# Refilling VectorE's queue further ahead in the w_out stages of an attention and relu² kernel, with a matmul product moved between the last ones of a stage

## Chip, cores, metric

One core of one Trainium2 chip. The metric is the device time of one execution in microseconds (us), lower is better.

## The reference, cut to what matters

```python
scores = (q @ k.transpose(0, 1, 3, 2)) / sqrt(64)      # B=8, H=12, S=448, D=64
attn   = (maximum(scores, 0) ** 2 / 448) @ v           # relu squared, no softmax
x      = attn.transpose(0, 2, 1, 3).reshape(3584, 768)
h      = x @ w_in                                      # 768 x 2048
g      = maximum(h, 0) ** 2
out    = g @ w_out                                     # 2048 x 768
```

## The kernel before

TensorE (PE) is kept busy with two matrix products, h = x @ w_in and out = g @ w_out, and the pieces of attention for later batches are laid between their matmuls. Both products use a seven-product scheme instead of eight (after Strassen). The other engines work for PE:

- ScalarE (ACT) turns scores into a tile `at` (relu), copies partial sums out of PSUM banks (`m1`, `u2`, `u3`), and copies attention's result into `xt`.
- VectorE (DVE) squares each `at`, does relu and square on parts of `g`, forms the sums `s1` to `s4` that the w_out products read, and the output sums `osb` = bank × constant + a copy.

Attention comes in units: seven tiles `at` of two heads' scores, then `av_unit`, 28 matmuls that need all seven squared. The schedule is fixed when the program is recorded. The recording code keeps a rough model of the time on PE (`at_pe`) and DVE (`at_ve`). DVE's urgent sums are issued where they are written; squares (`due`) and work on g (`due_g`) wait in lists, and `fill(until)` puts them into DVE's queue as long as the model says that they end before `until`. So **the order in DVE's queue is decided at recording time**, by the horizon given to `fill`:

```python
    def flush(rest=True):                  # put all that is left
        for d in (due, due_g) if rest else (due,):
            while d:
                put(d)

    def put(d):
        ready, cost, fn, _ = d.popleft()
        at_ve[0] = max(at_ve[0], at_pe[0], ready) + cost
        fn()

    def fill(until):
        for d in (due, due_g):
            while d and max(at_ve[0], at_pe[0], d[0][0]) + d[0][1] <= until:
                put(d)

    def av_unit():
        ...
        flush(rest=False)                  # squares left over: all of them now
        at_pe[0] += 2.65
        ...                                # 28 matmuls on the seven squared tiles
```

The w_out stage works in groups of two row tiles. A group has seven products of eight matmuls (8 × 384 columns), which add up in two banks, X and Y:

```python
            TAG = {"m1": "a", "u2": "b", "u3": "c"}
            ...
            def end7():                    # after product k = 4
                copy("u3")                 # ScalarE copies bank X
                plus(1, c1, "u3")          # VectorE: waits for that copy
                ...
            products = (                   # k = 0 .. 6
                (X, True, lambda: tile_of(rows[0])[:, LO], b11, end1),
                (Y, True, lambda: tile_of(rows[0])[:, HI], b21, end2),
                (X, False, lambda: ss[2], t2, end6),
                (Y, True, lambda: ss[1], t1, end5),
                (X, False, lambda: ss[3], t3, end7),
                (X, False, lambda: tile_of(rows[1])[:, HI], nt4, end4),
                (Y, False, lambda: ss[4], b22, end3))
            ...
                    if f == KH - 1:        # last matmul of product k
                        end()
                        fill(at_pe[0] + (1.7 if k in (1, 5) else 1.3))
        ...
        for n, ls in enumerate(lists):     # next group's first product
            for k in range(7):             #   between k = 4 and k = 5
                if k == 5 and n + 1 < len(lists):
                    steps += lists[n + 1][0]
                if k > 0 or n == 0:
                    steps += ls[k]
```

Product k = 5 adds to the bank that `copy("u3")` has to read first. In all groups but a stage's last, the next group's first product stands between them and hides the copy: the traced run lists two waits of w_out matmuls for a copy, of 0.64 us each, both in a stage's last group (at 312.11 and 386.96 us).

Of the kernel before, what the change touches and what calls it, by code (L numbers as in the profile page):

```python
# [11 lines left out]
FP32 = mybir.dt.float32  # L12
AF = mybir.ActivationFunctionType
ALU = mybir.AluOpType
# [3 lines left out]
def kernel(  # L18
# [9 lines left out]
    nc = tc.nc  # L28

    B, H, S, D = q.shape  # L30
    NT, DM = out.shape
# [10 lines left out]
    P = 128  # L42
# [6 lines left out]
    HALF = DM // 2  # L49
    NT_PAIR = 2 * S // P  # L50
    KH = NF // 2
# [4 lines left out]
    CO = 2.0 ** -42  # L56
# [109 lines left out]
    def sums_w1(i):  # L166


        op, c = divmod(i, 2)
        lo, hi = slice(0, NM // 2), slice(NM // 2, NM)  # L170
        a11, a12, a21, a22 = (w1[c][:, lo], w1[c][:, hi], w1[c + 2][:, lo],
                              w1[c + 2][:, hi])
        if op < 3:
            wsum[op, c] = late["ws"].tile(
                [P, NM // 2, 512], FP16, name=f"ws{op}{c}", tag=f"ws{op}{c}")
        if op == 0:
            nc.vector.tensor_add(wsum[0, c], a21, a22)
        elif op == 1:
            nc.vector.tensor_sub(wsum[1, c], wsum[0, c], a11)
        elif op == 2:  # L180
            nc.vector.tensor_sub(wsum[2, c], a12, wsum[1, c])
        else:
            nc.vector.tensor_sub(a21, a11, a21)
# [157 lines left out]
    at_pe = [0.0]  # L341
# [12 lines left out]
# [5 lines that stand above are left out]
    def now_ve(cost, lag=0.25):  # L359
        at_ve[0] = max(at_ve[0], at_pe[0] + lag) + cost  # L360
# [39 lines left out]
    def mm_tile(i=None):  # L400
        if i is None:
            mm_no[0] += 1
            i = mm_no[0] % len(big)
        return big[i].tile([P, 512], FP32, name="mm", tag="mm")
# [160 lines left out]
    def store(row, osb, c, eng, eng2=None):  # L565
        pr, tb = row
        for i in range(2):
            b, j = divmod(2 * tb + i, J)
            b += 2 * pr
            (eng2 if eng2 and i else eng).dma_start(  # L570
                out=out[b * S:(b + 1) * S, :].rearrange(
                    "(p j) d -> p j d", j=J)[:, j, c],
                in_=osb[64 * i:64 * i + 64, c])
# [26 lines left out]
        now_ve(0.6)  # L600
        op(to[i], x, y)  # L601

    def o_groups(groups):


        steps = []
        sets = [dict() for _ in groups]

        def group(n, rows, last):
            ss = sets[n]  # L610
            X: list = []
            Y: list = []
            c0, c1 = slice(0, HALF), slice(HALF, DM)
            osb: dict = {}
            keep: dict = {}

            def ahead(i, k=n):
                if k < len(groups) and k > 0:
                    flush_g(2 * B)
                if k < len(groups) and i not in sets[k]:  # L620
                    sums(i, groups[k], sets[k])

            TAG = {"m1": "a", "u2": "b", "u3": "c"}

            def copy(nm):
                t = late["m"].tile([P, S], FP32, name=nm, tag=TAG[nm])
                t = t[:, 0:HALF]
                nc.scalar.activation(out=t, in_=X[0][:, 0:HALF], func=AF.Copy, scale=CO)  # L628
                keep[nm] = t

            def plus(row, c, nm, cc=slice(0, HALF)):
                now_ve(0.5)
                nc.vector.scalar_tensor_tensor(  # L633
                    out=osb[row][:, c], in0=Y[0][:, cc], scalar=CO,
                    in1=keep[nm][:, cc], op0=ALU.mult, op1=ALU.add)

            def new_osb():
                for r in range(2):
                    osb[r] = late["osb"].tile([P, DM], FP32, name="osb", tag=f"osb{r}")

            def end1():
                copy("m1")

            def end2():
                new_osb()
                plus(0, c0, "m1")
                if last:
                    store(rows[0], osb[0], c0, nc.sync)

            def end6():  # L650
                copy("u2")
                ahead(3)

            def end5():
                ahead(4)

            def end7():
                copy("u3")
                plus(1, c1, "u3")
                if last:  # L660
                    store(rows[1], osb[1], c1, nc.sync)

            def end4():
                nc.scalar.activation(out=osb[1][:, c0], in_=X[0][:, 0:HALF],  # L664
                                     func=AF.Copy, scale=CO)
                if last:
                    store(rows[1], osb[1], c0, nc.gpsimd)
                else:
                    store(rows[1], osb[1], slice(0, DM), nc.sync)
                ahead(1, n + 1)  # L670
                ahead(2, n + 1)

            def end3():
                plus(0, c1, "u2")
                if last:
                    store(rows[0], osb[0], c1, nc.sync, nc.scalar)
                else:
                    store(rows[0], osb[0], slice(0, DM), nc.sync)

            products = (  # L680
                (X, True, lambda: tile_of(rows[0])[:, LO], b11, end1),
# [4 lines that stand above are left out]
                (X, False, lambda: tile_of(rows[1])[:, HI], nt4, end4),  # L686
                (Y, False, lambda: ss[4], b22, end3))

            def step(k, f):
                acc, fresh, left, right, end = products[k]  # L690

                def run():
                    if f == 0 and fresh and k != 3:
                        acc[:] = [mm_tile(n % 2)]
                    if f == 0 and k == 0:
                        ahead(1)
                        ahead(2)
                    nc.tensor.matmul(  # L698
                        acc[0][:, 0:HALF], lhsT=left()[:, f], rhs=right[:, f],
                        start=(fresh and f == 0),  # L700
                        stop=(f == KH - 1), skip_group_check=not fresh)
                    if f == KH - 1:
                        end()
                        fill(at_pe[0] + (1.7 if k in (1, 5) else 1.3))
                return run

            return [[(0.1625, step(k, f), ((2 if k == 5 else True) if f == 0 else False))
                     for f in range(KH)] for k in range(7)]

        def pre(i):  # L710
            sums(i, groups[0], sets[0])

        lists = [group(n, rows, rows == LAST) for n, rows in enumerate(groups)]
        for n, ls in enumerate(lists):
            for k in range(7):
                if k == 5 and n + 1 < len(lists):
                    steps += lists[n + 1][0]
                if k > 0 or n == 0:
                    steps += ls[k]
        return steps, pre  # L720

    def o_steps(pr):
        groups = [((pr, i), (pr, i + 1)) for i in (0, 2, 4)]
        if pr % 2 == 1:
            return o_groups(groups + [((pr - 1, 6), (pr, 6))])
        steps, pre = o_groups(groups)
        return steps + [(0.0, lambda: save((pr, 6)), False)], pre

    LAST = ((B // 2 - 2, 6), (B // 2 - 1, 6))
# [41 lines left out]
    T_G = NM * 0.1892  # L771
    T_H = NF * T_G
# [4 lines left out]
    events = []  # L777
# [34 lines left out]
            events.append((begin[pr] - 6 + i, lambda b=2 * pr, i=i: sums_x(b, i)))  # L812
    events.append((at0 + 0.3, lambda: visit([])))

    outs = [o_steps(pr) for pr in range(B // 2)]
    for i in (1, 2):
        events.append((2 * T_H - (3 - i) * T_G, lambda i=i: outs[0][1](i)))

    def pre(pr, i):
        def run():  # L820
            flush_g(2 * pr)
            outs[pr][1](i)
        return run

    steps = [(0.1892, None, False)] * 4 + f0[4:]
    for f in range(1, NF):
# [4 lines left out]
    for pr in range(1, B // 2):  # L831
        for b in (2 * pr, 2 * pr + 1):
            for i0 in (0, 4):
                extra: dict = {}
                if i0 and b % 2 == 0:
                    for p, i in ((9, 0), (9, 1), (13, 2), (13, 3)):
                        extra.setdefault(p, []).append(
                            lambda b=b, i=i: sums_x(b + 1, i))
                if i0 and b % 2 == 1:
                    extra[9] = [pre(pr, 1)]  # L840
                    extra[13] = [pre(pr, 2)]
                steps += h_period(b, i0, extra)
        steps += outs[pr][0]

    clock = 0.0
# [41 lines left out]
```

## Time and profile before

| | before |
|---|---|
| device time, median of the first 3 runs | 394.91 us (393.95 to 395.52) |
| span of the traced run | 394.3 us |
| PE busy / DVE busy / ACT busy | 370.6 / 275.7 / 251.1 us |
| PE waiting for squares | 8.2 us |
| span of the four w_out stages o0, o1, o2, last | 45.5, 50.8, 44.7, 41.8 us |

The page's head and its rows of slices (each digit is the busy share of a fortieth of the span, in tenths; PEclk is the granted clock, in tenths of full speed):

```profile
span 394.3 us, 8786 instructions
...
PE 370.6 (94%) x3592; PEld 231.8 (59%) x3592; DVE 275.7 (70%) x512; ACT 251.1 (64%) x374; POOL 107.3 (27%) x128
...
PE   8889999997989999999899999999698999999994
...
PEclk9899999999899999999999999999989999999999
```

Look at the three weak places of PE's row: a 7 and an 8 at slices 10 and 12 (stage o0), an 8 at 20 (stage o1), and a 6 and an 8 at 29 and 31 (stage o2). The clock's row dips at 11 and 30, just behind the 7 and the 6 (its other dip, at the second slice, lies near the program's start). PE is the bound everywhere else; DVE is idle 30% of the span, so the squares that PE waits for aren't late for lack of time.

### The profile page before, as it was taken

What the parts mean: (1) busy time and instruction counts of PE and PEld (TensorE: products, weight loads), DVE (VectorE), ACT (ScalarE), POOL (GpSimd) and SP (SyncE); (2) the same over time, 40 slices, a digit from 0 to 9 for tenths busy, and PEclk for the clock granted to TensorE, in tenths of its full rate; (3) what the DMA queues carried; (4) which work ended last, traced back from release to release, by engine and by line L of the source; (5) the groups of instructions that cost most, each with busy time, mean ns of one, the idle gap of its engine ahead of it and who ended that gap; (6) DMA issues with size and microseconds to landing.
All of it is one profiled execution on the core that took longest, in us unless ns stands there. A gap on an engine that the chain in (4) does not pass through costs nothing.

```text
span 394.3 us, 8786 instructions
## 1 busy us (share of the span) xinstructions
PE 370.6 (94%) x3592; PEld 231.8 (59%) x3592; DVE 275.7 (70%) x512; ACT 251.1 (64%) x374; POOL 107.3 (27%) x128
## 2 busy tenths in 40 slices
PE   8889999997989999999899999999698999999994
PEld 3444444443444678785455578786344488986662
DVE  1696567996555888795975758988735578996441
ACT  2797995785665898776465588786445686441120
POOL 8445423662441244413043044130000000000001
PEclk9899999999899999999999999999989999999999
DMA  8999999999997999869598999491230320001333
GB/s 121 197 204 204 205 193 145 150 148 116 149 113 152 165 91 111 100 88 72 95 124 123 196 136 93 73 118 25 47 82 6 81 77 2 2 0 38 99 98 89
DMA packets 121000, 42.65 MB, mean 108 GB/s; under 512 B 100800, under 2 KB 117600, under 8 KB 120960
## 3 DMA queue, kind: packets, MB, share of 16 engines
q0 software_dynamic: 82912, 23.01, 58.8%
q1 hardware_dynamic: 37968, 18.98, 25.4%
q8 instruction: 28, 0.46, 0.5%
q14 instruction: 12, 0.10, 0.1%
q10 hardware_dynamic: 80, 0.10, 0.1%
HBM read 45.61 MB, written 11.01 MB: 144 GB/s over the span
## 4 chain that ended last, share of the span: by engine, by line
PE 76%; DVE 8%; ACT 6%; DMA 4%; issue 2%; POOL 1%; POOLq 0%; ACTq 0%; DVEq 0%
PE mm L698 30%; PE mm L549 22%; PE slot L251 8%; PE mm L419 8%; PE slot L316 6%; DMA k<-in_k_dram 4%; DVE at L368 4%; ACT at L255 3%; DVE g L497 1%; DVE s L601 1%; ACT u L628 1%; PE slot L221 1%; DVE osb L633 1%; ACT m L485 1%; DVE g L490 1%
## 5 line engine op out<-in xcount | busy, mean ns | idle before, releaser
L255 ACT ACTIVATE at<-slot 128x896 f16<-128x896 f32 x168 | 146.2, 918 | 35.4 <-PE slot L251 35.4
L368 DVE TENSOR_TENSOR at<-at 128x896 f16<-128x896 f16 x168 | 98.8, 618 | 14.5 <-ACT at L255 14.4
L108 POOL DMA_DIRECT2D qs<-in_q_dram x36 | 35.4, 985 | 127.0 <-DMA qT<-qs 119.3
L698 PEld LDWEIGHTS <-s 128*128 128x128 f16 x448 | 42.6, 99 | 34.4 <-issue 6.7
L251 PE MATMUL slot<-qT,kT 64*64 64x448 f16 x756 | 59.2, 369 | 1.8 <-ACT kT L213 0.5
L549 PEld LDWEIGHTS <-w 128*128 128x128 f16 x576 | 54.5, 98 | 5.1 <-issue 4.7
L633 DVE SCALAR_TENSOR_TENSOR osb<-mm,u 128x384 f32<-128x384 f32 x28 | 15.6, 557 | 51.1 <-ACT u L628 39.4
L698 PEld LDWEIGHTS <-g 128*128 128x128 f16 x336 | 32.2, 100 | 27.9 <-issue 9.3
L549 PE MATMUL mm<-xt,w 128*128 128x224 f16 x432 | 48.1, 259 | 0.0
L549 PEld LDWEIGHTS <-ws 128*128 128x128 f16 x432 | 40.2, 98 | 6.6 <-issue 6.6
L316 PE MATMUL slot<-at,vt 64*64 64x448 f16 x588 | 34.9, 352 | 8.3 <-DVE at L368 8.2
L698 PE MATMUL mm<-b,g 128*128 128x384 f16 x224 | 42.0, 333 | 0.0
L698 PE MATMUL mm<-b,s 128*128 128x384 f16 x224 | 41.8, 330 | 0.0
L698 PE MATMUL mm<-t,s 128*128 128x384 f16 x224 | 39.5, 327 | 0.9 <-DVE s L601 0.9
L419 PE MATMUL mm<-xt,w 128*128 128x448 f16 x192 | 39.6, 353 | 0.3 <-ACT xt L279 0.3
L108 POOL DMA_DIRECT2D ks<-in_k_dram x36 | 35.1, 977 | 11.4 <-DMA b<-in_moe_w_out_dram 5.8
L251 PEld LDWEIGHTS <-kT 64*64 64x64 f16 x756 | 19.9, 107 | 30.3 <-issue 25.4
L570 POOL DMA_DIRECT2D out_dram<-osb x2 | 1.1, 565 | 129.2 <-ACT osb L664 129.2
L549 PE MATMUL mm<-x,ws 128*128 128x224 f16 x288 | 34.2, 259 | 0.9 <-ACT m L485 0.9
L628 ACT ACTIVATE u<-mm 128x384 f32<-128x384 f32 x28 | 13.8, 492 | 33.3 <-PE mm L698 32.1
L322 ACT ACTIVATE xt<-slot 128x896 f16<-128x896 f32 x21 | 19.3, 917 | 20.1 <-PE slot L316 20.1
L316 PEld LDWEIGHTS <-vt 64*64 64x64 f16 x588 | 18.0, 106 | 21.8 <-issue 13.4
(63 smaller groups left out, 408.1 us busy)
## 6 DMA issues: line engine op xcount, KB each, us to landing
out_dram<-osb SPq DMA_DIRECT2D x52, 192.0 KB, 3.1
vt<-in_v_dram POOLq DMA_DIRECT2D x24, 224.0 KB, 6.2
qs<-in_q_dram POOLq DMA_DIRECT2D x36, 112.0 KB, 4.1
ks<-in_k_dram POOLq DMA_DIRECT2D x36, 112.0 KB, 4.6
w<-in_moe_w_in_dram POOLq DMA_DIRECT2D x8, 384.0 KB, 11.6
b<-in_moe_w_out_dram POOLq DMA_DIRECT2D x4, 768.0 KB, 17.1
q<-in_q_dram POOLq DMA_DIRECT2D x6, 224.0 KB, 9.2
k<-in_k_dram POOLq DMA_DIRECT2D x6, 224.0 KB, 9.6
```

What stands on the lines that cost most here:

```text
L108: nc.gpsimd.dma_start(out=t[:, :, hh, :], in_=heads(src, n)[:, hh].rearrange("p (j d) -> p j d", d=D))
L221: nc.tensor.transpose(pss[i][64 * hh:64 * hh + 64, i, j * P:(j + 1) * P], src[:, hh, j * D:(j + 1) * D], ident)
L251: nc.tensor.matmul(ps[c, hh, 0:S], lhsT=kT[r, j, c], rhs=qT[r, :, c], start=True, stop=True)
L255: nc.scalar.activation(out=at, in_=ps[:, :, 0:S], func=AF.Relu, scale=SK)
L316: nc.tensor.matmul(ps[64 * hh:64 * hh + 64, hp, 0:S], lhsT=vt[r, hh, j * D:(j + 1) * D], rhs=at[r, hh, :], start=(j == 0), stop=(j == J - 1))
L322: nc.scalar.activation(out=xts[b][:, 2 * u:2 * u + 2, :], in_=ps[:, :, 0:S], func=AF.Copy, scale=CX)
L368: lambda: nc.vector.tensor_mul(at, at, at), 0))
L419: nc.tensor.matmul(cell[0][:, 0:S], lhsT=w1[f // 4][:, m, (f % 4) * P:(f % 4 + 1) * P], rhs=xts[b][:, m, :], start=(m == 0), stop=(m == NM ...
L549: nc.tensor.matmul(XY[s][y][:, r * Q:(r + 1) * Q], lhsT=left(k, i0 + 2 * s + r, m), rhs=right(k, m), start=(fresh and r == 0 and m == 0), ...
L628: nc.scalar.activation(out=t, in_=X[0][:, 0:HALF], func=AF.Copy, scale=CO)
L633: nc.vector.scalar_tensor_tensor(out=osb[row][:, c], in0=Y[0][:, cc], scalar=CO, in1=keep[nm][:, cc], op0=ALU.mult, op1=ALU.add)
L698: nc.tensor.matmul(acc[0][:, 0:HALF], lhsT=left()[:, f], rhs=right[:, f], start=(fresh and f == 0), stop=(f == KH - 1), skip_group_check=n ...
```

## The change

Its intent has three parts. (1) DVE's spare time in w_out stages goes to squares earlier: larger horizons. (2) In a stage's last group nothing hides the copy ahead of k = 5; six matmuls of the next h (one product of `h_period`) are moved there. (3) The very last group has no next h, so its product k = 5 goes to a free bank Z; VectorE adds up the output from Z, which was a ScalarE copy from X before, and makes one sum more, `u5`; and the last product is done in two halves of 192 columns with their own sums and stores. The diff, cut to its core:

```diff
 (in sums_w1: w_in's sums on DVE, now counted in the model)
+        now_ve(0.9)
-    def o_groups(groups):
+    def o_groups(groups, then):
-            TAG = {"m1": "a", "u2": "b", "u3": "c"}
+            TAG = {"m1": "a", "u2": "c", "u3": "d"}
+
+            AFTER = (1.9, 1.9, 2.8, 3.0, 3.0, 2.8, 1.9)
...
                         end()
-                        fill(at_pe[0] + (1.7 if k in (1, 5) else 1.3))
+                        fill(at_pe[0] + AFTER[k])
...
-                if k == 5 and n + 1 < len(lists):
-                    steps += lists[n + 1][0]
+                if k == 5:
+                    steps += lists[n + 1][0] if n + 1 < len(lists) else then
... (in o_steps)
+        if pr < B // 2 - 1:
+            p = 1 - pr % 2
+            then += periods[2 * pr + 2, 0][6 * p:6 * p + 6]
+            del periods[2 * pr + 2, 0][6 * p:6 * p + 6]
... (the last group: end7 also forms u5 = Y*CO + u2; end4's ScalarE copy is left out there)
             def end4():
+                if last:
+                    plus(1, c0, "u3", acc=Z)
+                    store(rows[1], osb[1], c0, nc.gpsimd)
+                    return
...
+            def end3_part(z):
+                h = HALF // 2
+                cc = slice(z * h, z * h + h)
+                c = slice(HALF + cc.start, HALF + cc.stop)
+                plus(0, c, "u5", acc=W, cc=cc)
+                store(rows[0], osb[0], c, nc.sync, nc.scalar)
...
+                if last and k == 5:
+                    acc, fresh = Z, True
...
+            if last:
+                ls[6] = [(0.0825, step3(z, f), False) for z in range(2) for f in range(KH)]
```

## The prediction

> **What bounds the kernel now.** TensorE (PE) is busy 94% of a 394.3 us span, so only its idle time and its slow time can be won. I first cut the span into stages by what PE runs. There are four w_out stages: o0 (86.3 to 131.8 us), o1 (175.7 to 226.5), o2 (270.8 to 315.5) and a last one (352.5 to 394.3). In them PE idles 3.2, 1.3, 5.5 and 5.2 us; in the three w_in stages between them 0.7, 1.1 and 0. So the reserve lies in the w_out stages. The list of PE's waits over the whole span names it (columns: total us, times, longest):
>
> ```profile
> PE slot L316 <- DVE at L368: 8.2, 15, 3.0
> ...
> PE mm L698 <- ACT u L628: 1.3, 2, 0.6
> ...
> PE mm L698 <- DVE s L601: 0.9, 1, 0.9
> ```
>
> L316 is attention's second product: it reads seven tiles `at`, each squared by VectorE (DVE, L368). PE's timeline in o2 shows one such unit:
>
> ```profile
> 280.68 0.95 PE L316 MATMUL slot<-at,vt 64*64 64x448 f16 x16
> 284.64 0.38 PE L316 MATMUL slot<-at,vt 64*64 64x448 f16 x4 [3.00 <-DVE at L368]
> 285.17 0.38 PE L316 MATMUL slot<-at,vt 64*64 64x448 f16 x4 [0.15 <-DVE at L368]
> 285.71 0.38 PE L316 MATMUL slot<-at,vt 64*64 64x448 f16 x4 [0.15 <-DVE at L368]
> 285.90 0.38 PE L251 MATMUL slot<-qT,kT 64*64 64x448 f16 x4
> 286.21 2.47 PE L698 MATMUL mm<-nt,g 128*128 128x384 f16 x8
> 288.47 2.19 PE L698 MATMUL mm<-b,s 128*128 128x384 f16 x8
> ```
>
> Undisturbed, a tile's four matmuls start 0.19 us after the previous tile's (unit at 177.16, whose next scores start at 178.48, 1.32 us later). This unit needs 5.22 us: 3.9 lost, more than the 3.3 us of idle shown, because single tiles run unpipelined. DVE's timeline says why the squares were late:
>
> ```profile
> 275.68 0.68 DVE L601 TENSOR_TENSOR s<-g,s 128x1024 f16<-128x1024 f16 x1
> 279.05 0.56 DVE L633 SCALAR_TENSOR_TENSOR osb<-mm,u 128x384 f32<-128x384 f32 x1 [2.68 <-ACT u L628]
> 279.52 0.61 DVE L368 TENSOR_TENSOR at<-at 128x896 f16<-128x896 f16 x1
> 280.05 0.62 DVE L497 TENSOR_TENSOR g<-g 128x896 f16<-128x896 f16 x1
> ...
> 283.97 2.76 DVE L368 TENSOR_TENSOR at<-at 128x896 f16<-128x896 f16 x5
> ```
>
> DVE idles 2.68 us at an output sum that waits for a ScalarE copy; squares whose inputs were long ready stand behind it, and behind 3.9 us of other work (280.05 to 283.97). It isn't short of time, its order is wrong.
>
> The third loss is in the last columns of slices of one us (PEclk is the first number after the busy times; 1.00 is full speed):
>
> ```profile
> 285.00:286.00 1.00, 0.69 (x15) 0.25 (x11) 1.00 (x3) 0.00 (x0) 0.00 (x0) 1.00 0.00 0
> 286.00:287.00 1.00, 1.00 (x12) 0.49 (x5) 0.72 (x2) 0.86 (x2) 0.00 (x0) 0.77 0.08 16
> 287.00:288.00 1.00, 1.00 (x5) 0.48 (x4) 0.10 (x1) 0.86 (x2) 0.00 (x0) 0.50 0.00 0
> 288.00:289.00 1.00, 1.00 (x5) 0.46 (x3) 0.52 (x1) 0.28 (x1) 0.00 (x0) 0.50 0.00 0
> 289.00:290.00 1.00, 1.00 (x4) 0.46 (x3) 0.00 (x0) 0.21 (x1) 0.00 (x0) 0.53 0.00 0
> 290.00:291.00 1.00, 1.00 (x8) 0.59 (x7) 0.30 (x1) 0.00 (x0) 0.00 (x0) 1.00 0.66 144
> ```
>
> After the stall PE runs at half clock for about 3.4 us. The same follows o0's first stall (98.8 to 102.1 us) and no other wait in a w_out stage.
>
> [...] Cutting the time before each drop into such windows, I count about 1.8 us idle in the window just ahead of both drops, and at most about 1.5 in windows that no drop followed; an estimate of the limit from this trace. [...] The trace gives 33.81 us for 208 of 384 columns, 162.5 each, and 96.7 ns each for 224; none of 192.
>
> **The change, part by part.** I took each engine's order in both builds, and worked forward with the durations above.
>
> *Squares earlier.* After each product the recording code fills DVE's queue up to a horizon, now 1.9 to 3.0 us in place of 1.3 to 1.7. DVE's instructions are the same in number apart from the last group; in o2's first unit the two pairs of squares and three operations on g now stand ahead of the waiting sum. Loss of each unit before, as start of the seventh tile less the start it would have at 0.19 us per tile, and what I expect after:
> - o0 first: 98.38 − 95.55 = 2.8. Its last two squares are still behind the sum that ends at 95.3; squares at 95.9 and 96.4, so 0.9 stays. Gain 1.9.
> - o0 second: 114.52 − 112.97 = 1.55; its squares precede the sum. Gain 1.5.
> - o1 second: 196.88 − 196.13 = 0.75. Gain 0.7.
> - o2 first: 3.9. DVE from 274.55: two squares 1.07, s3 0.6, three of g 1.4, s4 0.6, two squares 1.07, sum 0.5, s1 and s2 1.3, the last square 0.55: done near 281.7, wanted at 281.8. Gain 3.8.
> - o2 second: 301.78 − 299.67 = 2.1. The two squares behind the sum (298.2) end at 299.3, wanted at 299.5. Gain 2.1.
> - o1: the 0.9 us wait for a sum s: the g work ahead of it moves forward, s2 done near 190 and wanted at 191.2. Gain 0.9.
> Sum 10.9.
>
> *Clock.* If no window keeps 1.8 us of idle, both drops go. o0: eight matmuls took 2.67 us for 1.30 and eight scores 0.79 for 0.50, 1.65 lost. o2: 24 matmuls took 5.69 us for 3.9, 1.75 lost. Sum 3.4.
>
> *A product of the next h ahead of the stage's last pair.* In the last group of a stage nothing stands between the product that ScalarE must copy from its bank and the product that adds to that bank:
>
> ```profile
> 310.00 1.47 PE L698 MATMUL mm<-b,s 128*128 128x384 f16 x8
> 312.11 1.46 PE L698 MATMUL mm<-nt,g 128*128 128x384 f16 x8 [0.64 <-ACT u L628]
> ```
>
> Six h matmuls (6 × 0.097 = 0.58 us) now stand there, moved, not added: gain 0.64 in o2, 0.14 in o1 (gap ahead of 222.07). In o0 the move pulls two visits of attention together: 16 scores, with eight matmuls less between them. Scores have two slots, each freed by a 0.82 us ScalarE step; the queue there is u3, two steps, m1, two steps. I expect PE to wait about 0.3 and 0.6 us for slots, less the 0.14 saved: a loss of 0.7. Behind o1 the first copy m of h is done before ScalarE's `xt`, where PE waited some 0.3 us: gain 0.3. Sum 0.4.
>
> *Last group.* Its sixth product goes to a free bank and PE doesn't wait for the copy: 0.64. DVE gains one sum of 0.56 us beside PE. The last product is cut in two of 192 columns: [...] the final sum is half as wide, about 0.36 us for 0.56 (estimate): 0.2. Two more output transfers of half the size go out; the last still needs some 4 us from issue to the end as now (390.35 to 394.3). Sum 0.8.
>
> All: 10.9 + 3.4 + 0.4 + 0.8 = 15.5 us. For small new waits (a sum that now stands behind squares frees its bank later: in o1 near 187.2 us where PE wants it at 187.8) I take off 1.5: 14 us of 394.9 leaves 381.
>
> **Rivals.**
> 1. *ScalarE takes over as the limit.* For: with PE's stalls gone, its at steps, copies and `xt` come closer together; a DVE on time may only move the wait from squares to L255. Against: in o2 it works 23.6 of 44.7 us, in o0 29.3 of 45.5, and PE waits for at steps 0.5 us in all. If half of the unit losses came back as slot waits: 387.
> 2. *Queue order again.* More squares ahead of the sums make output sums late, and PE waits for banks in place of squares. For: the 0.6 us margin in o1. Against: in most groups the next group's product stands between. It would give back 2 to 4 us: 384.
> 3. *The clock still drops*, because 0.9 us in o0 and the slot waits at its end fall into one window. [...] Against: 0.9 is half of what came before. One drop costs 1.7: 383.
> 4. *Transfers bind once PE is faster.* Against: GpSimd's transfers of q mostly wait for a buffer (119 us behind transposes), and PE waits for no transfer after o0 begins. I give it no weight.
>
> **Range and chances.** 381 as centre. The high end takes rival 2 and one drop together, 386. The low end, 377.5, has all 15.5 us and the o0 slot waits away, with some gaps too short to be listed. Over 2% faster means below 387.0; that needs 8 of 15.5 us, and o2 alone has 8.3. Chances: faster 0.91, within 2% 0.08, slower 0.01.
>
> **What would show it.** PE's wait for squares falls from 8.2 to about 1 us, nearly all in o0's first unit; o2's units take about 1.3 us each; the clock is 1.00 in all of o0 and o2; o2 shrinks from 44.7 to about 36.5 us, o0 from 45.5 to about 41; the ScalarE copy wait of L698 is gone; at o0's end a new slot wait of about 0.9 us appears. DVE's busy time stays at 276 us. It is wrong if PE's waits reappear under L255 or L633, if half clock is still granted in o2 (then its cause isn't the idle before it), or if the w_in stages grow by what the w_out stages lost.

Where a cut is marked, statements on queues, on the clock and on the time of a matmul are taken out. The sum came to 10.9 + 3.4 + 0.4 + 0.8 = 15.5 us, less 1.5 is 14; the halves of the last product were counted as the same time on PE, and that isn't from this trace. "Such windows" are stretches of 3.413 us, as long as each stretch of half clock in that trace (98.80 to 102.21 and 286.53 to 289.95 us in the w_out stages); counted again in them, the idle time just ahead of the two drops is 1.85 and 1.82 us (1.93 ahead of a third, in the front), and 1.49 at most in the other windows up to the last matmul. "Unpipelined" is put for what the listing shows: a tile that had waited took 0.38 us, where tiles without a wait start 0.19 us apart. The prediction doesn't say from what it worked out the 0.36 us for a sum of half the width; the trace of after shows 0.36.

## The result

| | before | after |
|---|---|---|
| device time, median of 4 runs | 395.22 us (393.95 to 396.14) | 378.86 us (378.47 to 379.35) |
| ratio, 95% interval | | 0.9589 (0.9558 to 0.962) |
| span of the traced run | 394.3 us | 377.6 us |

A ratio is the mean time of one kernel's fast runs over that of the other's of the same rounds, so it is not quite the ratio of the medians quoted. All outputs are right.

The change made the kernel 4.1% faster. The page after, the same lines as before:

```profile
span 377.6 us, 8806 instructions
...
PE 363.5 (96%) x3600; PEld 231.3 (61%) x3600; DVE 278.6 (74%) x515; ACT 249.8 (66%) x373; POOL 107.1 (28%) x128
...
PE   7889999999999999999999999999999999999994
...
PEclk9999999999999999999999999999999999999998
```

The weak places in PE's row are gone, and so are the dips of the clock behind them. PE's waits, the two lines of attention's matmuls in the w_out stages (total us, times, longest):

```profile
PE slot L252 <- ACT at L256: 1.2, 4, 0.4
...
PE slot L317 <- DVE at L369: 0.5, 2, 0.4
```

The wait for squares went from 8.2 to 0.5 us, and no wait of the w_out products (now line L729) is listed any more, neither for a copy nor for a sum (a delay of 0.34 us in the last stage isn't in the list; it comes below). The first unit of o2, which took 5.22 us before, in PE's timeline after (start, duration, work):

```profile
270.57 1.48 PE L729 MATMUL mm<-b,g 128*128 128x384 f16 x8
271.97 0.38 PE L252 MATMUL slot<-qT,kT 64*64 64x448 f16 x4
272.33 1.55 PE L317 MATMUL slot<-at,vt 64*64 64x448 f16 x28
273.68 0.38 PE L252 MATMUL slot<-qT,kT 64*64 64x448 f16 x4
274.00 1.48 PE L729 MATMUL mm<-nt,g 128*128 128x384 f16 x8
```

All 28 matmuls run in one group, and the next scores start 1.35 us after the unit's start. DVE's timeline ahead of it shows the new order:

```profile
269.36 0.68 DVE L602 TENSOR_TENSOR s<-g,s 128x1024 f16<-128x1024 f16 x1
269.96 1.15 DVE L369 TENSOR_TENSOR at<-at 128x896 f16<-128x896 f16 x2
271.03 0.55 DVE L636 SCALAR_TENSOR_TENSOR osb<-mm,u 128x384 f32<-128x384 f32 x1
```

Two squares stand between the sum s and the output sum. When DVE gets to the output sum, ScalarE's last copy `u` (270.17 to 270.66 us) has been done for 0.37 us: the line has no wait in brackets, where before there were 2.68 us. The granted clock (after the busy times of the five engines) stays full:

```profile
270.00:274.00 4.00, 4.00 (x54) 1.95 (x53) 3.96 (x9) 3.38 (x6) 0.00 (x0) 1.00 0.53 102
274.00:278.00 4.00, 4.00 (x28) 2.26 (x24) 1.69 (x3) 2.03 (x3) 0.00 (x0) 1.00 0.30 62
```

**Where the time went.** I cut each trace at the first w_out matmul of each w_out stage, and at the last matmul of all. The first segment runs from the start of the span to o0; a segment such as "o0 to o1" has a w_out stage and the w_in stage after it (us):

| | front | o0 to o1 | o1 to o2 | o2 to last | last stage | tail | span |
|---|---|---|---|---|---|---|---|
| before | 86.28 | 89.27 | 95.05 | 81.76 | 37.36 | 4.58 | 394.3 |
| after | 84.39 | 84.84 | 93.02 | 73.28 | 36.93 | 5.14 | 377.6 |
| difference | −1.89 | −4.43 | −2.03 | −8.48 | −0.43 | +0.56 | −16.7 |

The front runs the same instructions in the same order on all engines in both. It took 83.25 to 86.28 us in the 14 traces; in the trace of before PE stood 1.7 us for the load of k, where it stood 0.7 in that of after, and half clock followed for 3.41 us (13.47 to 16.88). The only other traces with half clock in the front, e9 and e12 (both with the change), took 86.20 and 85.97. So its 1.89 us are chance of the one trace, which was a slow run besides: 396.39 us, above the four timed ones. The other five segments give 14.8 us (of which 1.46, in o0, are chance of this trace too, see e6); between the medians of before and after the later rounds show 15.05 and 14.69 us.

### The profile page after: what moved, and what is told of

Its sections match the earlier page's. It is cut to its first block, busy times and chain, and to the rows that moved or that the text cites. A ratio compares the mean times of both kernels' runs of the same rounds, so it can differ in the third digit from the quotient of the medians.

```text
span 377.6 us, 8806 instructions
## 1 busy us (share of the span) xinstructions
PE 363.5 (96%) x3600; PEld 231.3 (61%) x3600; DVE 278.6 (74%) x515; ACT 249.8 (66%) x373; POOL 107.1 (28%) x128
## 4 chain that ended last, share of the span: by engine, by line
PE 81%; ACT 6%; DVE 6%; issue 2%; DMA 2%; POOL 1%; POOLq 0%; ACTq 0%; DVEq 0%
PE mm L729 33%; PE mm L550 23%; PE slot L252 9%; PE mm L420 9%; PE slot L317 7%; ACT at L256 4%; DVE at L369 2%; DMA k<-in_k_dram 2%; PE slot L222 1%; DVE g L491 1%; ACT m L486 1%; DVE xt L283 1%; DVE s L602 1%; DVE g L498 0%; ACT qT L214 0%
## 5 line engine op out<-in xcount | busy, mean ns | idle before, releaser
L729 PEld LDWEIGHTS <-s 128*128 128x128 f16 x440 | 41.7, 98 | 32.0 <-issue 4.3
L252 PE MATMUL slot<-qT,kT 64*64 64x448 f16 x756 | 58.1, 360 | 2.6 <-ACT at L256 1.2
L550 PEld LDWEIGHTS <-w 128*128 128x128 f16 x576 | 54.4, 98 | 5.9 <-issue 5.4
L729 PEld LDWEIGHTS <-g 128*128 128x128 f16 x336 | 31.5, 98 | 24.0 <-issue 5.0
L729 PE MATMUL mm<-b,g 128*128 128x384 f16 x224 | 40.7, 326 | 0.0
L729 PE MATMUL mm<-b,s 128*128 128x384 f16 x216 | 39.6, 326 | 0.1
L729 PE MATMUL mm<-t,s 128*128 128x384 f16 x224 | 39.5, 326 | 0.0
L636 DVE SCALAR_TENSOR_TENSOR osb<-mm,u 128x384 f32<-128x384 f32 (+1 forms) x30 | 16.2, 541 | 31.2 <-ACT u L631 23.0
L252 PEld LDWEIGHTS <-kT 64*64 64x64 f16 x756 | 19.9, 104 | 31.1 <-issue 25.7
L317 PE MATMUL slot<-at,vt 64*64 64x448 f16 x588 | 32.2, 350 | 0.6 <-DVE at L369 0.5
L498 DVE TENSOR_TENSOR g<-g 128x896 f16<-128x896 f16 x48 | 29.7, 619 | 1.1 <-ACT g L501 0.2
L420 PEld LDWEIGHTS <-w 128*128 128x128 f16 x192 | 17.3, 98 | 19.1 <-issue 4.8
```

Source lines behind the costliest of these rows:

```text
L252: nc.tensor.matmul(ps[c, hh, 0:S], lhsT=kT[r, j, c], rhs=qT[r, :, c], start=True, stop=True)
L317: nc.tensor.matmul(ps[64 * hh:64 * hh + 64, hp, 0:S], lhsT=vt[r, hh, j * D:(j + 1) * D], rhs=at[r, hh, :], start=(j == 0), stop=(j == J - 1))
L420: nc.tensor.matmul(cell[0][:, 0:S], lhsT=w1[f // 4][:, m, (f % 4) * P:(f % 4 + 1) * P], rhs=xts[b][:, m, :], start=(m == 0), stop=(m == NM ...
L498: due_g.append((t, 0.54, lambda: nc.vector.tensor_mul(g, g, g), b))
L550: nc.tensor.matmul(XY[s][y][:, r * Q:(r + 1) * Q], lhsT=left(k, i0 + 2 * s + r, m), rhs=right(k, m), start=(fresh and r == 0 and m == 0), ...
L636: nc.vector.scalar_tensor_tensor(out=osb[row][:, c], in0=acc[0][:, 0:cc.stop - cc.start], scalar=CO, in1=keep[nm][:, cc], op0=ALU.mult, op ...
```

## The experiments

**Theory**: the gain is the order of VectorE's queue. PE no longer idles for squares, and with that the half clock behind the stalls goes too. **Rivals**: (a) the moved h product and the last group bring a real share; (b) the clock isn't a consequence of the stall but of something else in the stage; (c) any horizon that is long enough will do, so the numbers in `AFTER` don't matter. Each later table row is cut as above.

### One part at a time

e1: only the horizons (and the `now_ve(0.9)`), on the kernel before.

```diff
+            AFTER = (1.9, 1.9, 2.8, 3.0, 3.0, 2.8, 1.9)
-                        fill(at_pe[0] + (1.7 if k in (1, 5) else 1.3))
+                        fill(at_pe[0] + AFTER[k])
```

> The kernel before with the longer horizons for VectorE's queue alone (and the charge of 0.9 us for the weight sums), no moved product, old last group. Theory (queue order): the five late units and the late sum s of o1 go as in the changed kernel, 10.9 us by the prediction's list, and with them both half-clock stretches, 3.4 us: 14 us (13 to 15) below the kernel before; the waits of 0.64 us for the ScalarE copy stay in o2 and the last stage. Rival (ScalarE or banks were behind the squares): under 8 us.

e2: only the moved h product (the kernel after with old horizons, without `now_ve(0.9)`, and with the old last group).

```diff
-                        fill(at_pe[0] + AFTER[k])
+                        fill(at_pe[0] + (1.7 if k in (1, 5) else 1.3))
... (last group as before)
```

> The kernel before with the product of the next h moved ahead of a stage's last pair (and the tags of the copies renamed), old horizons, old last group. Theory: 0.64 us won in o2, 0.1 to 0.4 around o1's end, about 0.6 lost at the end of o0 by slot waits: within 0.6 us of the kernel before, the units as late as before and half clock twice. Rival (this part opened room for VectorE): over 2 us faster.

e3: only the last group (the kernel after with old horizons, without `now_ve(0.9)`, and with no moved product).

```diff
-                        fill(at_pe[0] + AFTER[k])
+                        fill(at_pe[0] + (1.7 if k in (1, 5) else 1.3))
-        if pr < B // 2 - 1:
+        if False:
```

> The kernel before with the changed last group alone (free bank, last product and its output in two halves). By the prediction: 0.8 us faster. By the trace of the changed kernel, in which PE's part of the last stage shrank by 0.43 us and the time from the last matmul to the end grew by 0.56: 0.1 us slower, so no difference that can be told (within 0.4 us).

Measured, with before at 393.87 us in the same rounds:

| | time | ratio to before (95%) | o0 to o1 | o1 to o2 | o2 to last | last stage | tail |
|---|---|---|---|---|---|---|---|
| e1 horizons | 379.32 | 0.962 (0.959–0.9651) | 84.11 | 93.20 | 74.07 | 37.72 | 4.51 |
| e2 h product | 394.31 | 0.9991 (0.9947–1.0035) | 88.53 | 94.87 | 80.30 | 37.36 | 4.53 |
| e3 last group | 393.93 | 0.9998 (0.9955–1.0041) | 87.80 | 95.06 | 81.71 | 36.58 | 5.10 |

The horizons alone give all of it that the timing can tell: 0.962, where the whole change measured 0.9589 in the first rounds and 0.9632 and 0.9622 in later ones. DVE has 512 instructions in e1 as before, so only their order changed. Rival (a) falls. The `now_ve(0.9)` went with the horizons in every run, so its share isn't known. What is left of PE's waits for w_out and squares in e1:

```profile
PE mm L701 <- ACT u L631: 1.3, 2, 0.6
...
PE slot L317 <- DVE at L369: 0.5, 2, 0.4
```

The squares' wait is as small as in the whole change; the copy's 1.3 us stay, because nothing was moved in front of it. The other two parts do what they should where they should, and lose it again elsewhere. The h product takes 0.79 us off "o2 to last" (74.07 in e1, 73.28 after) and 0.18 off "o1 to o2", and adds 0.73 to "o0 to o1" (84.11 to 84.84). The last group takes 0.78 off the last stage (37.36 to 36.58) and adds 0.52 to the tail.

### Is the clock a consequence of the stall?

e6: the kernel before, but PE does 14 matmuls on zeros ahead of the stalled unit of o2. They write the unit's own PSUM slot, which the unit's first matmuls overwrite. The stall stays; PE is merely not idle in it.

```diff
         ps = slot(FP32)
+        for _ in range(14 if n == 20 else 0):
+            nc.tensor.matmul(ps[:, 0, 0:S], lhsT=zeros[:, 0:P], rhs=zeros,
+                             start=True, stop=True)
```

> The kernel before with 14 dummy matmuls of 448 columns (2.6 us at full clock) ahead of o2's first unit, in the bank that the unit then overwrites. PE can't finish the unit sooner, because the squares come as late as before. Theory (half clock follows PE's idle time in a window): no half clock in o2, 1.7 us faster (1.2 to 2.0). Rival (the drop has another cause, or the dummy work costs time by itself): same time or slower, half clock still there.

Measured: 392.35 us, ratio 0.9952 (0.9918 to 0.9986); "o2 to last" went from 81.76 to 80.08. PE's timeline in e6, the zeros, the end of the unit, and the product after it:

```profile
277.42 2.81 PE L312 MATMUL slot<-zeros 128*128 128x448 f16 x14
...
282.45 0.38 PE L319 MATMUL slot<-at,vt 64*64 64x448 f16 x4 [0.15 <-DVE at L371]
...
282.95 1.47 PE L701 MATMUL mm<-nt,g 128*128 128x384 f16 x8
```

The unit still ends at the pace of the squares (its seventh tile starts 15.11 us after o2's first matmul in both traces), but the product behind it takes 1.47 us where it took 2.47 before. The slices around it, e6 first, then e2, which has the same stall without the zeros:

```profile
280.00:282.00 2.00, 1.58 (x26) 0.69 (x25) 1.97 (x5) 0.00 (x0) 0.00 (x0) 1.00 0.00 0
282.00:284.00 2.00, 1.85 (x19) 0.83 (x19) 1.47 (x3) 1.12 (x2) 0.00 (x0) 1.00 0.04 8
```

```profile
280.00:282.00 2.00, 0.36 (x4) 0.13 (x4) 1.97 (x4) 0.00 (x0) 0.00 (x0) 0.87 0.00 0
282.00:284.00 2.00, 2.00 (x18) 0.56 (x14) 1.73 (x4) 0.66 (x1) 0.00 (x0) 0.50 0.04 8
```

So PE's idleness brings the half clock, and rival (b) falls for o2: 1.68 us of the 8.48 there are clock. It is hardly luck of one trace: the six runs of e6 have a mean granted clock of 0.994 to 0.998 (on the average 0.995), the eleven of before in the same rounds 0.981 to 0.996 (0.988).

The drop in o0 is another matter. In e2, e3 and e6, which have before's order ahead of that place, the clock was 1.00 throughout o0, with the same stalls; "o0 to o1" took 87.80 and 87.81 us in e3 and e6, against 89.27 in the trace of before. And in e2 the half clock of o2 began in the midst of the stall, so that part of it fell on idle time: 80.30 is 81.76 less the 0.79 that the moved product gives in o2 and 0.67 more, so its half clock cost about 1.0 us (estimate: 1.68 − 0.67) in place of 1.68.

The traces show what decides it. In all 14, the changes of the clock lie a whole number of 3.413 us apart (in the trace of before, from the first full clock on, 2, 1, 24, 1, 54, 1 and 30 times that), and where this grid lies against the stage differs from run to run. I cut PE's idle time (with the ends of matmuls as the profile models them) on each trace's own grid, from the first full clock to the last matmul: 1514 windows. The seven with 1.82 to 2.86 us of idle were each followed by a window at half clock, and none of the others, with 1.60 us or less, was. The seven are all the drops there are in this stretch. o0's first stall left 1.85 us in one window in the trace of before, but at most 1.41, 1.60 and 1.29 in e2, e3 and e6. The length of a single gap doesn't tell it: in the trace of before the drop in o0 followed gaps of at most 1.0 us, that in o2 a gap of 3.0 us, and e6, which left 0.57 us idle in the stall of o2, shows no drop there. (Behind the last matmul it is less clear: a window of 1.85 us at e10's end was not followed by one at half clock.) In these traces a stall thus brings half clock or not, and costs more or less, as it happens to lie on the grid. It fits that before's runs scatter over 392.2 to 397.4 us, with a mean granted clock of 0.993 to 0.996 in those under 392.5 and of 0.986 or less in those over 395, the front's share included.

### Does the size of the horizon matter?

e7: the kernel after with one far horizon.

```diff
-            AFTER = (1.9, 1.9, 2.8, 3.0, 3.0, 2.8, 1.9)
+            AFTER = (5.0,) * 7
```

> The changed kernel with a horizon of 5.0 us after every product. Theory (VectorE's queue is a question of order in both directions): where many operations on g are pending, at the starts of o1, o2 and the last stage, they now stand ahead of a sum that frees a bank or feeds the next product; 1 to 4 us slower than the changed kernel, with waits of the w_out matmuls for sums or banks, and o0 (nothing pending on g) unchanged. Rival (the earlier the better): as fast as the changed kernel or faster.

Measured: 381.87 us (381.38 to 383.15), ratio 0.9693 (0.9661 to 0.9725) to before, against 378.84 for the kernel after in the same rounds: 3.0 us slower. "o1 to o2" grew by 1.63, "o2 to last" by 0.78, the last stage by 0.68; o0 stayed. New among PE's waits:

```profile
PE mm L729 <- DVE osb L636: 1.9, 3, 0.9
...
PE mm L729 <- DVE s L602: 1.0, 2, 0.7
```

At the start of o1, PE's timeline:

```profile
175.92 1.46 PE L729 MATMUL mm<-t,s 128*128 128x384 f16 x8 [0.66 <-DVE osb L636]
178.13 1.47 PE L729 MATMUL mm<-b,s 128*128 128x384 f16 x8 [0.75 <-DVE s L602]
```

The sum of the first wait ran on DVE at 175.32, behind nine operations on g that had begun at 171.14 (the first, the last, and the sum):

```profile
171.14 0.44 DVE L496 TENSOR_SCALAR g<-g 128x896 f16<-128x896 f16 x1
...
175.02 0.39 DVE L496 TENSOR_SCALAR g<-g 128x896 f16<-128x896 f16 x1
175.32 0.55 DVE L636 SCALAR_TENSOR_TENSOR osb<-mm,m 128x384 f32<-128x384 f32 x1
```

Rival (c) falls: too short a horizon puts squares behind sums that wait, too long a one puts sums that PE wants behind work with time to spare. This is the prediction's rival 2, and the values of the change avoid nearly all of it.

### What the change loses

Three places were left: 0.9 us in o0's first unit, the slot waits at o0's end, and the tail. o0's first unit after:

```profile
92.52 1.14 PE L317 MATMUL slot<-at,vt 64*64 64x448 f16 x20
94.03 0.38 PE L317 MATMUL slot<-at,vt 64*64 64x448 f16 x4 [0.37 <-DVE at L369]
94.56 0.38 PE L317 MATMUL slot<-at,vt 64*64 64x448 f16 x4 [0.15 <-DVE at L369]
```

The seventh tile starts at 94.56 instead of 92.52 + 6 × 0.19 = 93.66: the 0.9 of the prediction. And o0's end:

```profile
121.13 0.75 PE L550 MATMUL mm<-xt,w 128*128 128x224 f16 x6
122.14 0.38 PE L252 MATMUL slot<-qT,kT 64*64 64x448 f16 x4 [0.26 <-ACT at L256]
122.95 0.38 PE L252 MATMUL slot<-qT,kT 64*64 64x448 f16 x4 [0.43 <-ACT at L256]
```

e4: no moved product in o0.

```diff
-        if pr < B // 2 - 1:
+        if 0 < pr < B // 2 - 1:
```

> The changed kernel without the moved product at the end of o0 (kept in o1 and o2). Theory (two visits pulled together make PE wait for attention's slots): the waits of 0.26 and 0.43 us are gone, 0.4 to 0.7 us faster than the changed kernel. Rival (the move gives back the same at the start of the next w_in stage): no difference.

e5: the last product's halves are stored as one.

```diff
-                store(rows[0], osb[0], c, nc.sync, nc.scalar)
+                if z == 1:
+                    store(rows[0], osb[0], c1, nc.sync, nc.scalar)
```

> The changed kernel with the last product still in two halves but its output sent whole once both are summed (two transfers of 96 KB for four of 48 KB). Theory (the four small transfers take longer to issue and to land: the second on each queue can only be issued 0.64 us after the first, and lands 2.8 us after that against 2.1 to 2.4): 0.4 to 0.8 us faster than the changed kernel. Rival (the longer tail was chance): no difference, or slower, because the first half starts later.

e9: e4 and e5 together, and the squares put ahead of the sum that waits for u3.

```diff
                 copy("u3")
+                fill(at_pe[0] + 1.15)
                 plus(1, c1, "u3")
```

> The changed kernel without the moved product in o0, with the whole last transfer, and with VectorE's queue filled by up to 1.15 us after the ScalarE copy u3 is issued and before the sum that waits for it (for the 0.9 us left in o0's first unit). If the three add up: 0.55 + 0.55 + 0.9 = 2.0 us faster than the changed kernel. If squares ahead of the sum make banks late: less than 1 us.

e0: the kernel after once more, as the yardstick of these rounds.

> The changed kernel again, unchanged, as the common ground of this call: 378.9 us (378 to 380). If the front of the span up to o0's first matmul, 1.9 us shorter in its first trace, is chance and not the change, it lies anywhere between 84 and 87 us here.

Measured, with before at 394.07 us:

| | time | ratio to before (95%) | o0 to o1 | last stage | tail |
|---|---|---|---|---|---|
| e0 after again | 379.02 | 0.9632 (0.9609–0.9655) | 84.84 | 36.93 | 5.12 |
| e4 | 378.09 | 0.9605 (0.9588–0.9622) | 84.12 | 36.94 | 5.06 |
| e5 | 378.71 | 0.962 (0.9602–0.9637) | 84.84 | 36.93 | 4.78 |
| e9 | 377.53 | 0.9584 (0.9564–0.9604) | 83.20 | 36.94 | 4.77 |

The ratios of e0, e4 and e5 lie within each other's noise (only e9's is clear of e0's), so the segments decide. e4 wins 0.72 us in its segment, the loss of 0.7 that the prediction gave to this part. e5 wins 0.34 in the tail, less than the 0.4 to 0.8 expected. e9 wins another 0.92 in o0 over e4: in the segments the three add up, to 1.99 us of the 2.0 expected; in the medians, which take in the front, it is 1.49. DVE's and PE's timelines of e9 at that unit:

```profile
94.31 0.63 DVE L369 TENSOR_TENSOR at<-at 128x896 f16<-128x896 f16 x1 [0.18 <-ACT at L256]
94.85 0.55 DVE L636 SCALAR_TENSOR_TENSOR osb<-mm,u 128x384 f32<-128x384 f32 x1
```

```profile
94.33 1.52 PE L317 MATMUL slot<-at,vt 64*64 64x448 f16 x28
```

The square goes first, the sum finds its copy done, and the unit runs in one group. Where two squares stand to one sum in one queue was worth 0.9 us.

### Can it be pushed further, and do the halves help?

e10: e9, with the old horizons in the last stage (which has no attention) and Z's store issued by SyncE and ScalarE instead of GpSimd.

```diff
-            AFTER = (1.9, 1.9, 2.8, 3.0, 3.0, 2.8, 1.9)
+            AFTER = ((1.9, 1.9, 2.8, 3.0, 3.0, 2.8, 1.9) if groups[0][0][0] < B // 2 - 1 else
+                     (1.3, 1.7, 1.3, 1.3, 1.3, 1.7, 1.3))
-                    store(rows[1], osb[1], c0, nc.gpsimd)
+                    store(rows[1], osb[1], c0, nc.sync, nc.scalar)
```

> As the version with all three corrections (377.5 us), and the old horizons in the last stage alone (where no squares are left), and the transfer of the sum from the free bank issued on SyncE's and ScalarE's queues and no longer on GpSimd's. Theory: the last stage's product stream shrinks from 36.9 to 36.6 us as in the kernel with the last group alone, because no operations on g stand ahead of the sum s3; the tail shrinks from 4.8 to 4.5 us if the transfer on GpSimd's queue was the last to land, and stays if it wasn't. 0.3 to 0.7 us faster than all three.

e11: e10 with the last product whole (8 × 384 columns, one sum).

```diff
-                ls[6] = [(0.0825, step3(z, f), False) for z in range(2) for f in range(KH)]
+                ls[6] = [(0.1625, step3(0, f), False) for f in range(KH)]
... (h = HALF in step3 and end3_part)
```

> As the run before it, with the last product whole (eight matmuls of 384 columns, one sum, one pair of transfers). By the prediction's 0.2 us for the half sum: tail 0.2 us longer. If the halves cost as much as they give: the same.

e12: the kernel after in these rounds.

> The changed kernel, unchanged, for comparison in the same rounds: 379 us; the product streams of its stages 84.8, 93.0, 73.3 and 36.9 us as in its two traces, the front anywhere from 83 to 87.

Measured, with before at 393.53 us:

| | time | ratio to before (95%) | last stage | tail |
|---|---|---|---|---|
| e12 after again | 378.84 (378.35–380.89) | 0.9622 (0.959–0.9653) | 36.93 | 5.09 |
| e10 | 375.99 (375.69–376.13) | 0.9539 (0.9509–0.9568) | 36.57 | 4.26 |
| e11 | 375.99 (375.77–376.22) | 0.954 (0.9511–0.957) | 36.56 | 4.31 |

The old horizons give the last stage its 0.36 us back, in e10 and in e11. Those 0.36 us were the longer horizon's doing, as two lines of the last stage of the kernel after show, PE's product that waits for a sum (it could have started at 338.13 + 16 × 0.1625 = 340.73, and started at 341.07) and that sum on DVE behind an operation on g:

```profile
338.13 2.83 PE L729 MATMUL mm<-t,s 128*128 128x384 f16 x16
341.07 1.47 PE L729 MATMUL mm<-b,s 128*128 128x384 f16 x8
```

```profile
339.78 0.62 DVE L498 TENSOR_TENSOR g<-g 128x896 f16<-128x896 f16 x1
340.33 0.68 DVE L602 TENSOR_TENSOR s<-g 128x1024 f16<-128x1024 f16 x1
```

Before, nothing stood there: the same two products followed each other at 354.96 and 357.56. The tail lost another 0.51 us when GpSimd's two transfers, which had been issued at 372.25 and about 372.8, next to the very last ones, went to the other two queues. The halves of the last product bring nothing: e10 and e11 take the same time. **e10 beats both kernels**: 2.85 us (0.8%) faster than the change, in the same rounds, and 4.6% faster than before; e11 does the same with less code.

## Why the prediction was right

The predicted time was 381.0 us, the range 377.5 to 386.0; measured were 378.86. Point by point:

| step of the prediction | predicted gain | measured | from |
|---|---|---|---|
| o0: squares (1.9 + 1.5) and clock (1.65) | 5.05 | 5.16 | before to e1 |
| o0: the moved product | −0.7 | −0.73 | e1 to after |
| o1: squares 0.7, the sum s 0.9 | 1.6 | 1.85 | before to e1 |
| o1: the product, 0.14 + 0.3 | 0.44 | 0.18 | e1 to after |
| o2: squares (3.8 + 2.1) and clock (1.75) | 7.65 | 7.69 | before to e1 |
| o2: the product | 0.64 | 0.79 | e1 to after |
| last group | 0.8 | −0.13 | before to after, last stage and tail |
| taken off for small new waits | −1.5 | | see below |

- **Squares earlier**: right, unit by unit. Each unit's loss, and the time at which DVE would be done in the new order, could be read from the timeline before. Even the 0.9 us that stay in o0 came out.
- **Clock**: right in o2, where e6 measured 1.68 for the estimated 1.75. In o0 the 1.65 us are true of the one trace, but e2, e3 and e6 show that runs with the same stalls escape the drop. The step counted a chance event as if it came every time; the trace of before was 1.46 us longer there than e3 and e6. That the term is near the mark on the average is partly luck: from span and mean granted clock, the clock lost before's 31 runs of the later rounds 4.2 us on the average (1.6 to 7.5), and the 14 of the kernel after 1.1, so 3.1 less (an estimate, and an upper one, because some of it falls on idle time). The prediction's own figures for o2, 5.69 − 3.9, give 1.79, not 1.75.
- **The h product**: right in sign in all three stages and close in size; together −0.73 + 0.18 + 0.79 = +0.24 us, for 0.4 predicted. It is no gain that a timing shows (0.9991).
- **Last group**: the mis-sized term. 0.64 for the copy's wait was right (e3: 0.78 in the last stage). "0.2" for the halves was wrong: the 192 columns ran at 82.5 ns each in the traces of after and e10 (16 × 82.5 ns is 1.32 us, where 8 × 162.5 is 1.30), the half sum took 0.36 us as estimated, and the sum ended 0.18 us sooner after the stage's start in e10 than in e11, but only 0.04 of that is left at the end of the span; where the rest goes isn't shown. And the prediction overlooked that DVE gets three instructions more (512 to 515), not one, and two costs: 0.36 us by the longer horizon in a stage without squares, and 0.56 us more tail. The tail's step was "the last still needs some 4 us from issue to the end as now"; it took longer, with more and smaller transfers side by side. Their rows in the table of transfers (size, median us to landing), after and e10:

```profile
out_dram<-osb ACTq DMA_DIRECT2D x2, 48.0 KB, 2.8
out_dram<-osb SPq DMA_DIRECT2D x2, 48.0 KB, 2.7
```

```profile
out_dram<-osb ACTq DMA_DIRECT2D x2, 96.0 KB, 2.4
```

- **Small new waits**: 1.5 us were taken off, and the runs show 0.36 us of such waits, those of the last stage. In o1 none is listed. The measured time lies 2.1 us below the centre because of that over-caution and of the base: 394.9 us came from three runs, and before's medians in the later rounds are 393.5 to 394.1. The 0.9 us that the last group fell short went the other way.
- **Rivals of the prediction**: 1 (ScalarE) didn't come; waits for `at` on L252 are 1.2 us against 0.5, all of the difference at o0's end (1.0 us more, on L222, lies in the front, and e2, e3 and e6 have it as well). 2 (queue order) is real, but only at larger horizons (e7, 3.0 us) and in the last stage (0.36). 3 (the clock still drops): it is 1.00 in all of o0 and o2. 4 (transfers) got no weight and cost 0.5 us in the tail.

What stays open: whether the tail's loss is due to the size of the transfers, their number, or GpSimd's issue. e5 and e10 changed them in steps (5.12, 4.78 and 4.26 us), but the last step brought e10's store both to other queues and to an earlier time. In the kernel after, transfers of 48 KB landed in 2.7 to 2.8 us, and those of 96 KB in 2.3 to 2.5; but ScalarE's one of 96 KB in e5 took 2.8 as well, so size alone isn't shown to be the cause. And the idle time in a window that brings half clock is known only as between 1.60 and 1.82 us, from this kernel and its variants.

## What to carry to other kernels

When an engine with spare time is waited for, look at its queue before its busy share: the instruction ahead of the late one, and what that one waits for. Put work whose inputs are ready ahead of an instruction that will wait, but only as much as fits into the wait (here, squares moved ahead of one waiting sum won 0.92 us, e9); past it, the same move made the next consumer late (3.0 us lost, e7). And look at the granted clock behind a stall of PE: here half clock followed stalls that left 1.82 us or more idle in one window, and cost 1.0 (estimate) to 1.68 us in o2. Count it as a chance, not as a sum.
